# Chunk attention and two feed-forward layers on one core: 64x64 products four at a time, side work in short pieces behind steady work, GpSimd alone sums second weights, output banks rotate

## The chip, the cores and the metric

The kernel runs on one core of a Trainium2 chip. The metric is the time of one execution on the device in microseconds. Before the change it was 1657.01 us, the median of 3 runs (1655.79 to 1657.5).

## The reference

Attention is local: the 576 positions of each of 8 batches and 8 heads fall into chunks of 64, and a chunk attends to itself alone. Two feed-forward layers follow, on 4608 tokens of width 512, with 2048 hidden columns.

```python
scores = scale * np.matmul(q_c, k_c.transpose(0, 1, 2, 4, 3))   # chunks of 64 x 64
attn = np.exp(scores - max); attn = attn / (sum + 1e-09)
x = np.matmul(attn, v_c)                                         # -> [4608, 512]
h = x @ w_in;  r = np.maximum(h, 0.0);  x = (s * (r * r) + b) @ w_out
h = x @ w2_in; out = (h * (1.0 / (1.0 + np.exp(-1.702 * h)))) @ w2_out
```

The four weight matrices arrive as float64 and are turned into float32 on the chip ("decode").

## The kernel before

**Blocks and stages.** The tokens are cut into 9 blocks of 512 (`sizes`). Everything is kept transposed: features on the 128 partitions, 512 tokens in the free dimension. The first layer goes over the blocks one after the other; a block is a stage of `NS = 32` ticks, in which `gemm_in` (L479) makes 16 tiles of the hidden layer and `gemm_out` (L547), `LAG = 2` tiles behind, adds them into four accumulators in PSUM. Every product of float32 numbers is made of three matmuls on high and low parts (`split`, L94): low x high, high x high, high x low. A tile of the first layer has a steady chain behind its 12 matmuls: Relu on ScalarE (L499), s r^2 on VectorE (L500), the high part `gh` on ScalarE (L501), the low part `gl` on VectorE (L502).

**Attention.** While the first layer works on block j - 1, the four pairs of heads of block j are computed beside it (`Pair`, `plan_attention`). A pair's `steps` are a generator; `steps_at` calls `next` on it at given ticks: two 32x32 block transposes of q and k on VectorE (L252), 16 score products of 64x64 (L287), maximum and difference (L295, L296), exponential (L300), sum and quotient (L302 to L305), eight transposes (L261), 16 products with V (L271), split (L97). Float32 64x64 products take two matmuls each. Head 0 of a pair lies on partitions 0 to 63, head 1 on 64 to 127, in operands and in results. Blocks 0 and 1 are done ahead by `EarlyPair`, with transposes on TensorE, and its second product (L358) takes chunks two by two: input halves and output halves give all four combinations, and each input half has a PSUM bank of its own.

**Second weights.** The second layer runs block 0 in the same way, and the other eight two blocks at a time (`Halves`), by a scheme of seven products of quarter matrices instead of eight. For it sums and differences of quarters of the second weights are needed. `decode_second` turns a weight tile into float32 and stores it to DRAM; `sums` (L184) loads four quarters, makes four sums on GpSimd (L193 to L196), the high part on ScalarE (L198), the low part on GpSimd (L199), and stores both, 448 KB each, from SP (L204). This goes on beside the first layer in stages 2 to 8: every 13.3 ticks two decodes and two calls of `sums`.

**Halves.** The first products (`first`, L648) go through 8 tiles, with PSUM banks x (accumulator i % 4), d (the pool `at_ps`) and b; `quarter` (L668) makes the activated quarters. Then the seven output products (`second`, L742) run over 8 operands each, with both output tiles z = 0 and 1; their x banks are `acc2` and `acc3`. `operand` (L718) splits an operand (L730, L731), `result` (L763) adds, transposes and stores.

**What sets the order.** Every call is an item with a tick (`at`); the items are called in order of ticks (L885), and the framework then places the instructions on each engine's queue by a simulation of its own. A dependency without a semaphore (`tc.add_manual_dep(..., IN_ORDER)`) pins the order of two instructions on a queue. `schedule_with_timeline_sim=True` (L913) turns the simulation on. The descriptor room of GpSimd's transfers is 1024 bytes per partition (L904).

Of the kernel before, what the change touches and what calls it, by code (L numbers as in the profile page):

```python
# [11 lines left out]
ALU = mybir.AluOpType  # L12
# [12 lines left out]
FIRST_STEPS = (0, 0.6, 0.8, 1.1, 1.8, 2.4, 2.7, 3.6, 3.9, 4.5)  # L25
LAG = 2
# [18 lines left out]
def chunk_attention_two_ffn(ctx, tc, q, k, v, w1_in, w1_out, s, b, w2_in, w2_out, out):  # L45
# [33 lines left out]
    at_ps = ctx.enter_context(tc.tile_pool(name="at_ps", bufs=2, space=PSUM))  # L79
# [11 lines left out]
    wo_sums = dpool.tile([P, 7, KF // 2, 2, 2, P], F32, name="wo_sums")  # L91
    y_dram = [dpool.tile([P, KD, n], F32, name=f"y{j}") for j, n in enumerate(sizes)]
# [23 lines left out]
    def decode(st, m, c):  # L116
# [67 lines left out]
    def sums(kind, i, z):  # L184
# [3 lines left out]
        for t, (a, b) in ((i, one), (i + KF // 2, two)):  # L188
# [28 lines left out]
    heads = [slice(h * CH, (h + 1) * CH) for h in range(2)]  # L217

    class Pair:
# [20 lines left out]
        def load_v(self):  # L240
            self.v = apool.tile([P, self.nch, CH], F32, tag="vs", name="vs", bufs=HP)
            for off, m, bb, c in runs(self.j):
                for h in range(2):
                    rows = v[bb, 2 * self.hp + h, c * CH:(c + m) * CH, :]
                    nc.sync.dma_start(
                        out=self.v[h * CH:(h + 1) * CH, off:off + m, :], in_=rows.rearrange("(c p) d -> p c d", p=CH)
                    )

        def stage_qk(self):
            self.qt, self.kt = tmp("qt")[:, 0:self.n], tmp("kt")[:, 0:self.n]  # L250
            for t, src in ((self.qt, self.raw[0]), (self.kt, self.raw[1])):
                nc.vector.transpose(out=t.rearrange("p (u l) -> p u l", l=BK), in_=src)  # L252
            yield
            yield

        def turn(self, p):
            pt = tmp("pt")[:, 0:self.n].rearrange("p (c t) -> p c t", t=CH)
# [7 lines left out]
            return pt  # L265

        def second(self, pt):
            ps = at_ps.tile([P, self.n], F32, tag="at", name="xT")
            for c in range(self.nch):
                for r in heads:  # L270
                    nc.tensor.matmul(  # L271
                        out=ps[r, c * CH:(c + 1) * CH], lhsT=self.v[r, c, :], rhs=pt[r, c, :], start=True, stop=True
                    )
            return ps

        def split_x(self, ps):
            X[0, self.j, self.hp] = xh, xl = new_x()
            split(xh, xl, ps)

        def steps(self):  # L280
# [3 lines left out]
            ps = at_ps.tile([P, self.nch, CH], F32, tag="at", name="sc")  # L284
            for c in range(self.nch):
                for r in heads:
                    nc.tensor.matmul(  # L287
                        out=ps[r, c, :], lhsT=self.qt[r, c * CH:(c + 1) * CH], rhs=self.kt[r, c * CH:(c + 1) * CH],
                        start=True, stop=True,
                    )  # L290
# [4 lines left out]
            nc.vector.tensor_reduce(out=mx, in_=ps, axis=AX.X, op=ALU.max)  # L295
            nc.vector.tensor_tensor(  # L296
                out=p, in0=ps, in1=mx.unsqueeze(2).to_broadcast([P, self.nch, CH]), op=ALU.subtract
# [11 lines left out]
            turned = self.turn(p)  # L309
            yield  # L310
            ps = self.second(turned)
            yield
            self.split_x(ps)
            done[0, self.j] = done.get((0, self.j), 0) + 1

    class EarlyPair(Pair):
# [21 lines left out]
        def turn(self, p):  # L338
# [7 lines left out]
            return pt.rearrange("p (c h q) -> p c h q", h=2, q=CH)  # L346

        def second(self, pt):

            n = self.n // 2  # L350
            banks = (
                at_ps.tile([P, n], F32, tag="at", name="xT"),
                acc_ps.tile([P, n], F32, tag=f"acc{2 * (self.hp % 2) + 1}", name="xT"),
            )
            for c in range(self.nch // 2):
                for e, ps in enumerate(banks):
                    for h, r in enumerate(heads):
                        nc.tensor.matmul(  # L358
                            out=ps[r, c * CH:(c + 1) * CH],
                            lhsT=self.early.v[c][heads[e], (2 * self.hp + h) * D:(2 * self.hp + h + 1) * D],  # L360
                            rhs=pt[heads[e], c, h, :], start=True, stop=True,
                        )
            return banks

        def split_x(self, banks):
            X[0, self.j, self.hp] = x = new_x()
            xh, xl = (t.rearrange("p (c e t) -> p c e t", e=2, t=CH) for t in x)
            for e, ps in enumerate(banks):
                split(xh[:, :, e, :], xl[:, :, e, :], ps.rearrange("p (c t) -> p c t", t=CH))
            if self.j == 0:  # L370
                first_x.update((i.engine, i) for i in nc.cur_bb.bb.instructions[-2:])
            elif self.hp == HP - 1:
                marks.update((("x", i.engine), i) for i in nc.cur_bb.bb.instructions[-2:])
# [543 lines left out]
```

## Time and profile before

| | |
|---|---|
| median of 3 runs | 1657.01 us |
| the profiled execution | 1660.28 us |
| its span, first to last instruction | 1658.5 us |
| TensorE (PE) busy | 1604.2 us, 97% |
| VectorE (DVE) busy | 1149.3 us, 69% |
| ScalarE (ACT) busy | 747.0 us, 45% |
| GpSimd (POOL) busy | 266.9 us, 16% |
| mean granted clock of TensorE | 0.990 |
| chain that ended last | PE 77%, DVE 8%, DMA 4% |

A matmul's booked time reaches from its start to its modelled end, and the next one starts before that end: a full matmul is booked 0.39 us. In the rows, L12 is line 12 of the kernel before; PEld is TensorE's weight load; SPq, POOLq are the parts of engines that issue transfers. A time in brackets with an arrow is how long the engine sat idle just before, and who ended that.

### The profile page before, as it was taken

How to read it: one execution, taken by the hardware profiler on the slowest of the kernel's cores; microseconds unless marked ns; L12 is line 12 of the kernel's file. 1: busy time of each engine (PE TensorE's matmuls, PEld its weight loads, DVE VectorE, ACT ScalarE, POOL GpSimd, SP SyncE). 2: the span in 40 equal slices, each digit the busy share in tenths (PEclk: the TensorE clock that was granted, in tenths of full speed). 3: DMA queues.
4: the chain of work that ended last, by engine and by line, in shares of the span. 5: the costliest groups of instructions: out<-in, count | busy, mean ns of one | idle time of the engine just before them, and what ended most of it. 6: DMA issues, size and time to landing. Idle time of an engine off the chain costs nothing.

```text
span 1658.5 us, 24595 instructions
## 1 busy us (share of the span) xinstructions
PE 1604.2 (97%) x8928; PEld 1312.8 (79%) x8928; DVE 1149.3 (69%) x1836; ACT 747.0 (45%) x1258; POOL 266.9 (16%) x294
## 2 busy tenths in 40 slices
PE   6879999999999999999999999999999999999998
PEld 5758887778788878888888888878887888788876
DVE  5876666867687775777757543579568946984685
ACT  3768543333333333333345532456345525653552
POOL 1322101333223223233333000000001000100000
PEclk9889999999999999999999999999999999999999
DMA  9435445656455554646456441676868686767654
GB/s 229 114 102 162 121 132 131 146 132 163 122 141 145 143 136 132 156 128 155 117 160 216 135 135 45 188 239 221 206 195 266 181 221 207 255 183 218 219 192 77
DMA packets 398345, 272.19 MB, mean 164 GB/s; under 512 B 255376, under 2 KB 345488, under 8 KB 398224
## 3 DMA queue, kind: packets, MB, share of 16 engines
q1 hardware_dynamic: 390800, 249.64, 55.0%
q0 software_dynamic: 5120, 16.78, 3.0%
q10 hardware_dynamic: 2304, 4.20, 0.7%
q8 instruction: 71, 1.16, 0.3%
q14 instruction: 50, 0.41, 0.1%
HBM read 209.72 MB, written 60.82 MB: 163 GB/s over the span
## 4 chain that ended last, share of the span: by engine, by line
PE 77%; DVE 8%; DMA 4%; SPq 3%; ACT 3%; issue 2%; POOL 2%; POOLq 0%; DVEq 0%; ACTq 0%
PE acc L562 19%; PE h L487 18%; PE x L658 11%; PE x L753 11%; PE d L658 5%; PE d L753 5%; PE b L658 3%; PE b L753 3%; SPq L235 2%; PE sc L287 1%; PE xT L271 1%; DVE gl L502 1%; DVE r L500 1%; DVE pt L261 1%; ACT gh L501 1%
## 5 line engine op out<-in xcount | busy, mean ns | idle before, releaser
L487 PE MATMUL h<-xh,wi 128*128 128x512 f32 x1280 | 402.7, 396 | 13.5 <-ACT r L517 5.4
L562 PE MATMUL acc<-gh,wo 128*128 128x512 f32 x1152 | 354.8, 394 | 6.0 <-ACT gh L96 3.7
L487 PEld LDWEIGHTS h<-xh,wi 128*128 128x128 f32 x1280 | 240.3, 190 | 66.3 <-ACT r L517 6.3
L562 PEld LDWEIGHTS acc<-gh,wo 128*128 128x128 f32 x1152 | 215.5, 189 | 53.0 <-ACT gh L96 4.1
L487 PE MATMUL h<-xl,wi 128*128 128x512 f32 x640 | 251.2, 394 | 0.0
L562 PE MATMUL acc<-gl,wo 128*128 128x512 f32 x576 | 220.3, 392 | 3.8 <-DVE gl L502 3.8
L501 ACT ACTIVATE gh<-r,sb 128x512 fp32r<-128x512 f32 x112 | 80.9, 723 | 184.4 <-DVE r L500 184.1
L500 DVE SCALAR_TENSOR_TENSOR r<-r,sb 128x512 f32<-128x512 f32 x112 | 103.9, 928 | 64.3 <-ACT r L499 63.8
L502 DVE SCALAR_TENSOR_TENSOR gl<-r,sb,gh 128x512 fp32r<-128x512 f32 x112 | 107.3, 959 | 57.2 <-ACT gh L501 57.1
L487 PEld LDWEIGHTS h<-xl,wi 128*128 128x128 f32 x640 | 121.7, 190 | 25.9
L562 PEld LDWEIGHTS acc<-gl,wo 128*128 128x128 f32 x576 | 108.1, 188 | 28.6 <-DVE gl L502 6.2
L128 POOL TENSOR_TENSOR wm<-wm,wc 128x512 int32<-128x512 int32 x52 | 75.7, 1459 | 338.6 <-DVE wm L124 176.9
L730 ACT ACTIVATE op<-wo 128x512 fp32r<-128x512 f32 x128 | 79.5, 630 | 79.4 <-PE d L753 25.9
L680 DVE TENSOR_TENSOR wo<-wo,r 128x512 f32<-128x512 f32 x96 | 66.0, 691 | 63.0 <-ACT r L679 62.6
L753 PE MATMUL x<-op,wi 128*128 128x512 f32 x432 | 104.4, 389 | 0.0
L658 PE MATMUL x<-xh,wi 128*128 128x512 f32 x320 | 99.5, 391 | 3.1 <-DVE wo L677 3.1
L261 DVE STREAM_TRANSPOSE pt<-p 32x256 f32<-32x256 f32 x224 | 97.7, 436 | 3.9
L597 POOL DMA_DIRECT2D xr<-y x32 | 17.3, 540 | 506.3 <-DVE op L731 262.8
L679 ACT ACTIVATE r<-wo 128x512 f32<-128x512 f32 x96 | 60.8, 633 | 76.8 <-DVE wo L677 76.0
L753 PEld LDWEIGHTS x<-op,wi 128*128 128x128 f32 x432 | 81.1, 188 | 16.9
L731 DVE TENSOR_TENSOR op<-wo,op 128x512 fp32r<-128x512 f32 x128 | 85.2, 680 | 7.4 <-ACT op L730 6.0
L198 ACT ACTIVATE wst<-wst 128x896 fp32r<-128x896 f32 x32 | 30.5, 953 | 128.1 <-POOL wst L196 83.5
(145 smaller groups left out, 2780.1 us busy)
## 6 DMA issues: line engine op xcount, KB each, us to landing
wi<-wo_sums SPq DMA_DIRECT2D x112, 512.0 KB, 3.9
wi<-wi_sums SPq DMA_DIRECT2D x96, 512.0 KB, 3.7
wst<-in_moe_w_out SPq DMA_DIRECT2D x32, 512.0 KB, 4.6
wi_sums<-wst SPq DMA_DIRECT2D x32, 448.0 KB, 3.6
wo_sums<-wst SPq DMA_DIRECT2D x32, 448.0 KB, 3.5
wst<-in_moe_w_in SPq DMA_DIRECT2D x24, 512.0 KB, 5.0
y<-ost SPq DMA_DIRECT2D x36, 256.0 KB, 3.3
xr<-y POOLq DMA_DIRECT2D x32, 256.0 KB, 6.1
```

The lines of the kernel that those rows point to most:

```text
L128: nc.gpsimd.tensor_tensor(out=t, in0=t, in1=c.bitcast(I32), op=ALU.add)
L261: nc.vector.transpose(out=pt[r.start + ek * BK:r.start + (ek + 1) * BK, :, eq * BK:(eq + 1) * BK], in_=p[r.start + eq * BK:r.start + (eq + ...
L487: nc.tensor.matmul(out=ps, lhsT=w_[:, kk, :], rhs=x_, start=kk == 0 and a == 0, stop=kk == KD - 1 and a == 2,)
L500: nc.vector.scalar_tensor_tensor(out=r, in0=r, scalar=s_ap, in1=r, op0=ALU.mult, op1=ALU.mult)
L501: nc.scalar.activation(out=gh, in_=r, func=AF.Identity, bias=b_ap)
L502: nc.vector.scalar_tensor_tensor(out=gl, in0=r, scalar=b_ap, in1=gh.bitcast(F32), op0=ALU.add, op1=ALU.subtract)
L562: nc.tensor.matmul(out=acc[m], lhsT=l_, rhs=r_, start=i == 0 and a == 0, stop=i == KF - 1 and a == 2)
L658: nc.tensor.matmul(out=self.ps[key], lhsT=l_, rhs=r_, start=start and k == 0 and a == 0, stop=k == HK - 1 and a == 2, skip_group_check=not ...
L680: nc.vector.tensor_tensor(out=g, in0=h, in1=r, op=ALU.mult)
L730: nc.scalar.activation(out=hi, in_=src, func=AF.Copy)
L731: nc.vector.tensor_tensor(out=lo, in0=src, in1=hi.bitcast(F32), op=ALU.subtract)
L753: nc.tensor.matmul(out=self.ps[key], lhsT=l_, rhs=r_, start=start and i == 0 and a == 0, stop=i == HF - 1 and a == 2, skip_group_check=not ...
```

## The change

- **Products.** `quarters` gives the 16 products of a pair in an order in which four follow each other on the four combinations of input half and output half. Half of the chunks (e = 1) get the other output half; V is loaded with its halves exchanged for them. Scores and xT lie in halves (`left`, `right`) of two banks that are held for the whole kernel (`at_banks`). The early pairs' scores are done the same way.
- **Side work.** The transposes of a pair become single steps (q, k) and four steps of two; `PAIR_STEPS` gives 13 ticks. Every instruction that a `step` issues on ScalarE or VectorE gets a dependency without a semaphore on the latest steady instruction (Relu, s r^2, gh, gl) whose tick has passed.
- **Decode.** The square on ScalarE and the multiplication with the mask come before GpSimd's add instead of after it; the add is last.
- **sums.** The high part is made by GpSimd, the low part in four pieces, and both stores are issued by GpSimd.
- **Banks.** The d banks are the two of `at_banks` in turn; the x banks of `first` and of the outputs begin at accumulator 0 or 2 in turn (`turn`).
- **The end.** In the last pair of blocks the last product is ordered by output tile: from operand 2 on, first all of z = 0, then all of z = 1.

```diff
+PAIR_STEPS = (-2, -1.5, -1, 1, 1.9, 2.2, 3, 3.7, 4.2, 4.7, 5.2, 8, 8.5)
-    at_ps = ctx.enter_context(tc.tile_pool(name="at_ps", bufs=2, space=PSUM))
+    at_ps = ctx.enter_context(tc.tile_pool(name="at_ps", bufs=1, space=PSUM))
+    at_banks = at_ps.tile([P, 2, NB_MAX], F32, name="at")
     (decode)
+        square = low.bitcast(F32)
+        nc.scalar.activation(out=square, in_=high.bitcast(F32), func=AF.Square)
+        nc.vector.scalar_tensor_tensor(out=m, in0=square, scalar=TINY * TINY, in1=m, op0=ALU.is_ge, op1=ALU.mult)
+        yield
         nc.gpsimd.tensor_tensor(out=t, in0=t, in1=c.bitcast(I32), op=ALU.add)
-        nc.scalar.activation(out=c, in_=high.bitcast(F32), func=AF.Square)
-        yield
-        nc.vector.scalar_tensor_tensor(out=m, in0=c, scalar=TINY * TINY, in1=m, op0=ALU.is_ge, op1=ALU.mult)
     (sums)
-        nc.scalar.activation(out=hi, in_=q[:, 1:8, :], func=AF.Copy)
-        nc.gpsimd.tensor_tensor(
-            out=q[:, 1:8, :].bitcast(F32R), in0=q[:, 1:8, :], in1=hi.bitcast(F32), op=ALU.subtract
-        )
+        nc.gpsimd.tensor_copy(out=hi, in_=q[:, 1:8, :])
+        for t0, t1 in ((0, 2), (2, 4), (4, 6), (6, 7)):
+            nc.gpsimd.tensor_tensor(
+                out=q[:, 1 + t0:1 + t1, :].bitcast(F32R), in0=q[:, 1 + t0:1 + t1, :], in1=hi[:, t0:t1, :].bitcast(F32),
+                op=ALU.subtract,
+            )
-            nc.sync.dma_start(out=to[:, :, part, :], in_=src)
+            nc.gpsimd.dma_start(out=to[:, :, part, :], in_=src)
     (products of a pair)
+    left, right = at_banks[:, :, 0:NB_MAX // 2], at_banks[:, :, NB_MAX // 2:NB_MAX]
+    def quarters(nch):
+        for i in range(nch // 2):
+            for e in range(2):
+                for h in range(2):
+                    yield e, i, e * (nch // 2) + i, h, heads[h], heads[h ^ e]
     (Pair.load_v)
+                for e in range(2):
+                    a, z = max(off, e * half), min(off + m, (e + 1) * half)
+                    for h in range(2) if a < z else ():
+                        rows = v[bb, 2 * self.hp + h, (c + a - off) * CH:(c + z - off) * CH, :]
+                        nc.sync.dma_start(
+                            out=self.v[heads[h ^ e], a:z, :], in_=rows.rearrange("(c p) d -> p c d", p=CH)
+                        )
     (Pair.second; the scores likewise, into left)
-            ps = at_ps.tile([P, self.n], F32, tag="at", name="xT")
-            for c in range(self.nch):
-                for r in heads:
+            for e, i, c, h, r, other in quarters(self.nch):
+                nc.tensor.matmul(
+                    out=right[r, e, i * CH:(i + 1) * CH], lhsT=self.v[other, c, :], rhs=pt[other, c, :],
+                    start=True, stop=True,
+                )
     (Pair.turn: a yield after every two transposes; plan_attention)
-            steps_at(((o - 2, 3), (o + 1, 1), (o + 2, 4), (o + 8, 1), (o + 8.5, 1)), pr.steps)
+            steps_at([(o + t, 1) for t in PAIR_STEPS], pr.steps)
     (EarlyPair)
+        def room_scores(self):
+            return right if self.j == 0 and self.hp % 2 else left
     (gemm_in, first layer from block 2 on)
+        def steady(d, engine):
+            served.append((NS * j + 2 * i + d, engine, nc.cur_bb.bb.instructions[-1]))
             nc.scalar.activation(out=r, in_=ps, func=AF.Relu)
+            steady(2, ACT)
             nc.vector.scalar_tensor_tensor(out=r, in0=r, scalar=s_ap, in1=r, op0=ALU.mult, op1=ALU.mult)
+            steady(2.2, DVE)
     ...  (gh: 2.6, gl: 2.8)
     (Halves)
+            self.turn = j // 2 * HK % KD
+            if bank == "d":
+                self.ps[key] = at_banks[:, next(turns) % 2, :]
+                return
-                self.bank(key, BANK[m], f"acc{i % KD}")
+                self.bank(key, BANK[m], f"acc{(self.turn + i) % KD}")
-                    self.bank(key, BANK[m], f"acc{HK + z}")
+                    self.bank(key, BANK[m], f"acc{(self.turn + z) % KD}")
+                    if self.last and n == len(OUT_ORDER) - 1 and i >= 2:
+                        for z in range(2):
+                            at(base + 4 * n + 1 + 1.5 * z + 0.25 * (i - 2), self.second, n, i, (z,))
     (the loop over the items)
+        for ins in traced[n:] if f.__name__ == "step" else ():
+            first = next((g for u, e, g in reversed(served) if u <= t and e == ins.engine), None)
+            if first is not None:
+                tc.add_manual_dep(ins, first.name, IN_ORDER, reason="behind the tile before")
```

## Rows read from the trace of the kernel before

**Rows 1.** Page, part 1: busy time, share of the span, instructions of each engine.

```profile
PE 1604.2 (97%) x8928; PEld 1312.8 (79%) x8928; DVE 1149.3 (69%) x1836; ACT 747.0 (45%) x1258; POOL 266.9 (16%) x294
```

**Rows 2.** Busy time by stretches; columns as the first line says.

```profile
core 0: us, PE busy (x) PEld busy (x) DVE busy (x) ACT busy (x) POOL busy (x), PEclk, DMA share, GB/s
40.00:120.00 80.00, 64.14 (x515) 50.44 (x515) 64.26 (x108) 55.06 (x102) 24.13 (x17) 0.87 0.40 110
200.00:640.00 440.00, 429.72 (x2834) 349.53 (x2832) 320.67 (x519) 164.30 (x263) 115.82 (x129) 1.00 0.56 140
320.00:360.00 40.00, 37.77 (x266) 30.33 (x265) 24.90 (x36) 13.16 (x21) 13.14 (x15) 0.96 0.59 144
1120.00:1160.00 40.00, 40.00 (x178) 33.15 (x177) 40.00 (x68) 24.98 (x45) 0.01 (x1) 1.00 0.68 220
280.00:860.00 580.00, 572.60 (x3770) 469.55 (x3770) 429.23 (x681) 210.79 (x335) 184.67 (x206) 1.00 0.54 138
```

**Rows 3.** Waits of PE, 200:900 and 1000:1660: us in total, times, longest.

```profile
PE h L487 <- ACT r L499: 4.2, 3, 2.2
PE acc L562 <- DVE gl L502: 3.8, 3, 1.4
PE acc L562 <- ACT gh L501: 2.1, 3, 0.9
...
PE x L753 <- DVE wo L680: 5.8, 4, 1.5
```

**Rows 4.** Timeline of PE at 346 and 118: start us, us, instructions.

```profile
346.29 1.15 PE L271 MATMUL xT<-pt,vs 64*64 64x64 f32 x32
347.37 0.73 PE L487 MATMUL h<-xh,wi 128*128 128x512 f32 x2
...
118.22 0.69 PE L358 MATMUL xT<-pt,wo 64*64 64x64 f32 x32
118.85 0.73 PE L562 MATMUL acc<-gh,wo 128*128 128x512 f32 x2
```

**Rows 5.** Groups by line, PE: count | busy us, mean ns | idle before.

```profile
L287 PE MATMUL sc<-kt,qt 64*64 64x64 f32 x1152 | 45.7, 232 | 0.5 <-ACT kt L336 0.5
...
L271 PE MATMUL xT<-pt,vs 64*64 64x64 f32 x896 | 33.8, 221 | 0.0
```

**Rows 6.** Timeline of all engines at 337 to 339, and of VectorE at 269.

```profile
337.52 0.95 ACT L198 ACTIVATE wst<-wst 128x896 fp32r<-128x896 f32 x1 [9.94 <-POOL wst L196]
...
338.54 2.10 POOL L199 TENSOR_TENSOR wst<-wst 128x896 fp32r<-128x896 f32 x1 [1.06 <-ACT wst L198]
338.99 2.21 DVE L500 SCALAR_TENSOR_TENSOR r<-r,sb 128x512 f32<-128x512 f32 x1 [5.90 <-ACT r L499]
...
339.00 0.73 PE L487 MATMUL h<-xh,wi 128*128 128x512 f32 x2 [2.23 <-ACT r L499]
...
269.79 3.59 DVE L261 STREAM_TRANSPOSE pt<-p 32x256 f32<-32x256 f32 x8
```

**Rows 7.** Waits of all engines: us in total, times, longest.

```profile
ACT wst L198 <- POOL wst L196: 83.5, 18, 9.9
```

**Rows 8.** Groups by line, POOL: count | busy us, mean ns | idle before.

```profile
L199 POOL TENSOR_TENSOR wst<-wst 128x896 fp32r<-128x896 f32 x32 | 68.1, 2129 | 50.0 <-ACT wst L198 50.0
L194 POOL TENSOR_TENSOR wst<-wst 128x128 f32<-128x128 f32 x32 | 21.2, 663 | 83.9 <-DMA wst<-w_wi 37.5 <-DMA wst<-w_wo 35.7 <-DMA ks<-in_k 6.7
...
L597 POOL DMA_DIRECT2D xr<-y x32 | 17.3, 540 | 506.3 <-DVE op L731 262.8 <-ACT r L679 136.5 <-DVE wo L147 39.1
```

**Rows 9.** Timeline at 1133 to 1136, PE and VectorE.

```profile
1133.11 3.11 PE L753 MATMUL x<-op,wi 128*128 128x512 f32 x13
...
1133.44 0.68 DVE L731 TENSOR_TENSOR op<-wo,op 128x512 fp32r<-128x512 f32 x1
```

**Rows 10.** Timeline of the end: VectorE, then SP's issues.

```profile
1650.81 1.40 DVE L772 STREAM_TRANSPOSE ost<-x 128x512 f32<-128x512 f32 x2 [6.60 <-PE x L753]
...
1651.56 4.14 SPq L776 DMA_DIRECT2D out<-ost  x8
```

More of the change, by code (lines that the diff above doesn't have):

```diff
@@ L1 @@
+from itertools import count
 import concourse.bass as bass
@@ L241, in load_v @@
             self.v = apool.tile([P, self.nch, CH], F32, tag="vs", name="vs", bufs=HP)
+            half = self.nch // 2
             for off, m, bb, c in runs(self.j):
[L243 to L247, printed above, removed]
+                for e in range(2):
[5 more added lines that the diff above has]
+                        )
         def stage_qk(self):
@@ L264, in turn, with split_x @@
                         )
-            return pt
+                    yield
+        def room_scores(self):
+            return left
         def second(self, pt):
-            ps = at_ps.tile([P, self.n], F32, tag="at", name="xT")
-            for c in range(self.nch):
-                for r in heads:
[L271 to L278, printed above, removed]
+            for e, i, c, h, r, other in quarters(self.nch):
[3 more added lines that the diff above has]
+                )
+        def split_x(self):
+            X[0, self.j, self.hp] = x = new_x()
+            split(*(t.rearrange("p (e n) -> p e n", e=2) for t in x), right)
         def steps(self):
@@ L283, in steps @@
             yield
[L284 to L290, printed above, removed]
+            ps = self.room_scores().rearrange("p e (c t) -> p e c t", t=CH)
+            for e, i, c, h, r, other in quarters(self.nch):
+                nc.tensor.matmul(
+                    out=ps[other, e, i, :], lhsT=self.qt[r, c * CH:(c + 1) * CH], rhs=self.kt[r, c * CH:(c + 1) * CH],
+                    start=True, stop=True,
+                )
             yield
@@ L294, in steps @@
             p = tmp("p")[:, 0:self.n].rearrange("p (c t) -> p c t", t=CH)
-            nc.vector.tensor_reduce(out=mx, in_=ps, axis=AX.X, op=ALU.max)
+            by_bank = mx.rearrange("p (e c) -> p e c", e=2)
+            nc.vector.tensor_reduce(out=by_bank, in_=ps, axis=AX.X, op=ALU.max)
             nc.vector.tensor_tensor(
-                out=p, in0=ps, in1=mx.unsqueeze(2).to_broadcast([P, self.nch, CH]), op=ALU.subtract
+                out=p.rearrange("p (e c) t -> p e c t", e=2), in0=ps,
+                in1=by_bank.unsqueeze(3).to_broadcast([P, 2, self.nch // 2, CH]), op=ALU.subtract,
             )
@@ L308, in steps @@
             yield
-            turned = self.turn(p)
+            yield from self.turn(p)
+            self.second(self.pt)
             yield
-            ps = self.second(turned)
-            yield
-            self.split_x(ps)
+            self.split_x()
             done[0, self.j] = done.get((0, self.j), 0) + 1
@@ L345, in turn, with room_scores @@
             nc.vector.tensor_copy(out=pt, in_=ps)
-            return pt.rearrange("p (c h q) -> p c h q", h=2, q=CH)
+            self.pt = pt.rearrange("p (c h q) -> p c h q", h=2, q=CH)
+            yield
+        def room_scores(self):
+            return right if self.j == 0 and self.hp % 2 else left
         def second(self, pt):
             n = self.n // 2
[L351 to L354, printed above, removed]
+            if self.j == 0:
+                self.ps = (
+                    h_ps.tile([P, n], F32, tag="h", name="xT"),
+                    acc_ps.tile([P, n], F32, tag=f"acc{2 * (self.hp % 2) + 1}", name="xT"),
+                )
+            else:
+                self.ps = right[:, 0, :], right[:, 1, :]
             for c in range(self.nch // 2):
-                for e, ps in enumerate(banks):
+                for e, ps in enumerate(self.ps):
                     for h, r in enumerate(heads):
+                        of = h ^ (c >= self.nch // 4)
                         nc.tensor.matmul(
@@ L360, in second, with split_x @@
                             lhsT=self.early.v[c][heads[e], (2 * self.hp + h) * D:(2 * self.hp + h + 1) * D],
-                            rhs=pt[heads[e], c, h, :], start=True, stop=True,
+                            rhs=pt[heads[e], c, of, :], start=True, stop=True,
                         )
-            return banks
-        def split_x(self, banks):
+        def split_x(self):
             X[0, self.j, self.hp] = x = new_x()
[L367 to L373, printed above, removed]
+            xh, xl = (t.rearrange("p (c e t) -> p e c t", e=2, t=CH) for t in x)
+            if self.j:
+                split(xh, xl, right.rearrange("p e (c t) -> p e c t", t=CH))
+                if self.hp == HP - 1:
+                    marks.update((("x", i.engine), i) for i in nc.cur_bb.bb.instructions[-2:])
+                return
+            for e, ps in enumerate(self.ps):
+                split(xh[:, e], xl[:, e], ps.rearrange("p (c t) -> p c t", t=CH))
+            first_x.update((i.engine, i) for i in nc.cur_bb.bb.instructions[-2:])
     class Early:
@@ L504, in gemm_in @@
             )
+            steady(2.8, DVE)
         else:
@@ L580, in chunk_attention_two_ffn @@
     HF, HK = KF // 2, KD // 2
+    turns = count()
     def minus(to, one, two):
@@ L585, in chunk_attention_two_ffn, with __init__ @@
     class Halves:
-        def __init__(self, j, base):
-            self.j, self.base = j, base
+        def __init__(self, j, base, last):
+            self.j, self.base, self.last = j, base, last
+            self.turn = j // 2 * HK % KD
             self.x, self.w, self.g, self.op, self.ps, self.kept = {}, {}, {}, {}, {}, {}
@@ L740, in chunk_attention_two_ffn, with second @@
         n_ops = 0
-        def second(self, n, i):
+        def second(self, n, i, sides=(0, 1)):
             m = OUT_ORDER[n]
-            hi, lo = self.op.pop((n, i))
+            hi, lo = self.op[n, i]
             w = self.wo[n, i // 2]
-            for z in range(2):
+            for z in sides:
                 key = "out", z, BANK[m]
```

17 lines of the change are left out of this document (10 added, 7 removed).

## The prediction, written before the changed kernel ran

> **What bounds the kernel now.** I read the page's first part, then the busy time by stretches, then who waited for whom, and last the timeline around each loss. TensorE is busy for 97% of the span [rows 1], and a dense stretch without attention work holds 178 full matmuls in 40 us, 0.2247 us each [rows 2]. So TensorE sets the end: an edit pays only if it takes time out of TensorE's stream or closes a hole in it. The holes: 15.9 us idle in 40:120, at a granted clock of 0.87; 10.3 us in 200:640, and within it a clock of 0.96 in 320:360 [rows 2]; and four waits of 1.5 us late in the kernel [rows 3]. VectorE's 69% is no bound as a mean, but in 1120:1160 it is busy for all of the 40 us [rows 2]; there it decides what a closed hole is worth.
>
> **A. 64x64 products four at a time.** Before, the products run two at a time: 32 matmuls (16 products, two passes each) stand between a start at 346.29 and the next full matmul at 347.37, 1.08 us [rows 4]. The second product of the early pairs already uses all four quarters of the array: its 32 at 118.22 take 0.69 instead of 1.15 us, and the next full matmul starts at 118.85, 0.63 later [rows 4]. This is the shape that the change gives to every product; the difference is 0.45 us a block. There are 896 / 32 = 28 blocks of xT and 1152 / 32 = 36 of scores, of which 8 belong to early pairs [rows 5]: 56 blocks in the dense part, each in TensorE's own stream with nothing beside it, so **-25.2 us**. Bounds: 0 (they run as pairs after all; a loss is out, as count and kind of instructions stay) and -25.2. I take the full value, since the row has the same operand sizes.
>
> The Trainium skill speaks against it ("TensorE: Matmul & The Clock Gate", section "Wait — 56ns, not 53.3ns?"): starts of matmuls never come closer than about 25 ns, however small they are. By it 32 starts need 0.8 us and A shrinks to some -7 us (an estimate). The row differs: 32 in 0.69 us, with 0.22 for the last, is 15 ns between starts [rows 4, 5]; I go by the row.
>
> What A needs beside it costs nothing. V's halves change partitions, so `load_v` issues at most six loads a pair where it issued four: two more of SP's half microseconds (D) in the 20 us of a pair, while SP hands 64 stores of 448 KB to GpSimd. Scores and xT get one buffer each, in halves of the same two banks, and are used again a pair later: 7 ticks of 3 us (a stage of 32 ticks is 384 full matmuls and eight blocks, 95 us), where max, subtract and split hold them for 0.7 us each. Even if the banks are guarded whole, a reader waits for one block, and TensorE is back 7 ticks later.
>
> **B. Side work: `sums` on GpSimd alone, decode without a round trip, short pieces.** The timeline of the largest hole shows the chain [rows 6]: ScalarE's copy L198 stands 9.94 us at the head of its queue for GpSimd's sums; the Relu L499 comes behind it; then VectorE's L500 takes 2.21 us because GpSimd's L199 (2.10) runs across it; and TensorE waits 2.23 us. In all, L198 waited 83.5 us for GpSimd [rows 7]. After the change no instruction of `sums` or of the second weights' decode makes ScalarE or VectorE wait for GpSimd's result, so this blocking goes. The other kind is a run of VectorE steps, eight transposes for 3.59 us ahead of steady work [rows 6]; they become four pieces with steady work ordered ahead of them.
>
> The size: 10.3 us idle, 0.04 x 40 = 1.6 for the clock [rows 2], and the hidden part of nine waits [rows 3] (a full matmul is booked 0.39 busy and spaced 0.225, so 0.16 each, 1.4): 13.3. The new order starts with the first tile of stage 2, so the holes around that tile (240:280) are not all in its reach; I leave 2.3 of them. **-11 us**, bounds 0 and -13.3.
>
> What is late next is GpSimd. A `sums` step costs it four small sums of at most 0.66 [rows 8], 2.6 us; the subtraction in four pieces, 3.2 (L199's 2.13, and 0.36 for each extra start: a small sum has the columns of a seventh of L199, 0.30); one copy that no row shows on this engine, between 0.3 (a seventh of L199) and 2.13 (L199 itself, the same columns with two inputs): I take 2.1, the same shape; and two stores. A 256 KB transfer of 128 rows is issued in 0.54 [rows 8]; these have 896 rows, so between 0.54 and seven times that, 3.8; I take 1. Sum 9.9 us. Every 13.3 ticks (39 us) bring two `sums` and two decodes (an add, about 1.5 by its columns against L199, and an issue): 2 x 9.9 + 2 x 2.0 = 24 us. It fits, and at 3.8 an issue it is 35. Behind a store on GpSimd stand the next add and the next sums; their readers come stages later. GpSimd's hold on VectorE stays as long in sum, in pieces of 0.5 to 0.8 us, the copy at worst 2.1.
>
> The new order adds no semaphore, but a step of a pair now stands behind the Relu, square, gh or gl of the tile due before it. Behind the step stand the pair's later steps, and TensorE waits for them at two points: scores come 2.5 ticks after the second transpose of q and k, xT 2.8 ticks after the last transpose of p, 7 to 8 us of cover for steady operations of 0.75. VectorE is 429 of 580 us busy in 280:860 [rows 2], 79% once the stretch is 36 us shorter: the cover holds.
>
> **C. Output banks rotate.** Where first products give way to second ones, TensorE waits four times, 5.8 us in all, for L680 [rows 3], the last reader of the second output bank. With the banks alternating the outputs take the two that were read two tiles earlier. But VectorE is full behind it: the tightest operand that I find is ready at 1133.44 + 0.68 = 1134.12, and the matmul that reads it is the last of the 13 from 1133.11, near 1135.83 [rows 9]: 1.7 us of slack, of which 1.5 will be used. It fits barely. **-5.2 us**, bounds 0 (VectorE takes it back) and -6.4 (with 0.16 hidden each).
>
> **D. The end.** VectorE's last two transposes end at 1652.2, and SP's last eight issues take 4.14 us from 1651.56, 0.52 each [rows 10]; z = 1 gets its turn after the four of z = 0, near 1653.6. With z = 0 finished 18 matmuls (4 us) earlier its issues are over, and z = 1 starts near 1652.3. **-1.3 us**, bounds 0 and -2.1 (four issues).
>
> **E. The first 120 us.** The eight blocks of early scores get shorter by 0.45 us or, at half clock, twice that, and the first weights' decode loses ScalarE's square behind GpSimd's add. But 15.9 us of idle there [rows 2] belong to many waits in a row. Bounds -5 (a third of the idle) and +3 (one hole like the largest, with its clock); **-1.5**.
>
> Sum: -25.2 - 11 - 5.2 - 1.3 - 1.5 = -44.2. The profiled execution took 1660.28 us (span 1658.5 and 1.8 around it), so 1616.1 in its terms; the median of the runs shown is 1657.01, 3.3 less: **1613 us**.
>
> **The rivals.**
> 1. The holes move: pieces and order make the pair's own chain late, and VectorE takes C back; B and C bring nothing. For it: VectorE's full stretch, and 79%. Against: 7 us of cover. 1613 + 16 = 1629.
> 2. The change doesn't do what it says: four products, two from different row halves into one bank, fall back to pairs. For it: the block at 118.22 gives each bank one row half only. Against: the pairs before already write one bank from both. 1613 + 25 = 1638. The Trainium skill ("TensorEngine Tiling (Array Packing)", "Gotcha 1: PSUM Pressure") says that row tiles can't use one bank at the same moment; no row here shows such a loss.
> 3. Starts stay nearer to the pairs' 30 ns, (1.15 - 0.22) / 31, than to 15 [rows 4]: halfway, A is halved, 1626.
> 4. GpSimd becomes the bound, and the kernel slower: a store of 896 rows holds its queue, sums come late, staging rooms stay taken, SP stands before them, and q and k land late. Without its four stores a period needs 2 x 7.9 + 2 x 2.0 = 20 of 39 us, so it decides from 4.8 us a store; at 6.5 the period is 46, and 16 of them cost 112: 1725. Against: seven times the row is 3.8.
>
> **How the numbers follow.** Forecast 0.61, rival 1 0.17, rival 2 0.06, rival 3 0.05, rival 4 0.07, better than 1600 (every upper bound) 0.04. The range 1600 to 1638 holds the forecast with its bounds and rivals 1 to 3. A measurement of this kernel tells 0.2%, 3.3 us, from no change: faster 0.93, within 0.02, slower 0.05, the last two from rival 4.
>
> **What would show it.** A: groups of 32 small products near 0.7 us. B: no wait of ScalarE for GpSimd in `sums`, and under 3 us of TensorE's waits in 280:860. C: no wait at the four changes and none for operands soon after. D: four issues behind the last transpose. Wrong if a block keeps 1.1 us, if GpSimd needs over 4 us for a store, or if TensorE waits for the operands of scores or xT.

## The result and the profile after

The changed kernel takes 1680.69 us, the median of 4 runs (1676.39 to 1685.72), against 1656.4 for the kernel before, now with a fourth run: a ratio of 1.0146 [1.013, 1.0163], 1.5% slower, and the whole interval lies above 1. 1613 had been forecast. The profiled execution has a span of 1674.4 us, 15.9 more than before.

Where the 15.9 us arise can be read from TensorE's own milestones, the first matmul of a stage in the timeline: up to stage 2 it is 1.6 us later than before (209.35 against 207.74); stages 2 to 8, the first layer with attention and side work beside it, take 755.0 us instead of 730.2 (+24.8); from there to the last matmul it is 704.4 instead of 713.5 (-9.0); and behind the last matmul 5.56 instead of 7.06 (-1.5). One stretch made the change slower, and it is the one in which most of the gain was to lie.

The page's first line of the changed kernel, for [rows 1]:

```profile
PE 1588.8 (95%) x8928; PEld 1287.1 (77%) x8928; DVE 1158.0 (69%) x1832; ACT 716.2 (43%) x1222; POOL 398.9 (24%) x486
```

GpSimd works half as long again as before, and is idle for 76% of the span all the same. The busy time by stretches, for [rows 2]; the columns are engines' busy us with their instructions, then the granted clock:

```profile
320.00:340.00 20.00, 18.29 (x127) 15.19 (x128) 17.90 (x30) 4.85 (x8) 7.31 (x11) 0.83 0.47 114
280.00:860.00 580.00, 545.60 (x3681) 436.78 (x3680) 415.78 (x664) 175.48 (x289) 282.06 (x357) 0.98 0.49 131
```

In 280:860 TensorE idles 34.4 us where it idled 7.4, and GpSimd is busy for 282 of 580 us, 49%, so it has time left. TensorE's waits in 200:930 of the changed kernel (us in total, times, longest), for [rows 3]:

```profile
PE acc L607 <- DVE gl L546: 10.1, 11, 1.6
...
PE acc L607 <- ACT gh L544: 8.6, 6, 4.6
...
PE acc L607 <- DVE ost L615: 7.6, 6, 3.1
...
PE h L528 <- ACT r L540: 6.3, 4, 2.3
...
PE at L296 <- DVE pt L285: 6.0, 5, 2.3
```

With two small ones they are 41.1 us in 34 waits, against 10.1 in 9 before [rows 3]. All of them wait for ScalarE or VectorE. What held those two stands in the waits of all engines over the same stretch, sorted by time:

```profile
ACT wc L125 <- DMA wst<-in_moe_w_in: 75.3, 13, 13.5
DVE wm L126 <- DMA wst<-in_moe_w_in: 70.3, 10, 16.0
ACT wc L125 <- DMA wst<-in_moe_w_out: 50.0, 11, 9.5
POOL wi_sums L213 <- issue: 43.1, 15, 5.0
DVE wm L126 <- DMA wst<-in_moe_w_out: 40.6, 12, 6.4
POOL wo_sums L213 <- issue: 34.6, 13, 4.0
```

L125 and L126 are the decode's first instructions on ScalarE and VectorE. They waited 236 us for their loads. In the same stretch of the kernel before, one wait for such a load is listed:

```profile
DVE wm L121 <- DMA wst<-in_moe_w_in: 0.2, 1, 0.2
```

Why the loads come late is in SP's waits (whole kernel):

```profile
SPq L119 <- DMA wi_sums<-wst: 57.2, 8, 13.0
...
SPq L113 <- DMA wo_sums<-wst: 51.9, 10, 10.8
```

SP holds the decode's load (L113, L119) until a store of `sums` has landed. A load goes into a staging room (`staged`, three in all, and one call of `sums` takes two), and the room is free only when the store out of it is through. These are 109.1 us; the kernel before has 10.8 of the same kind:

```profile
SPq L108 <- DMA wo_sums<-wst: 6.2, 8, 1.7
...
SPq L114 <- DMA wi_sums<-wst: 4.6, 8, 0.7
```

One event from the timeline of all engines (start, us, instruction, and in brackets the idle time ahead of it with its releaser):

```profile
679.90 2.31 SPq L256 DMA_DIRECT2D qs<-in_q  x3
...
685.91 0.90 POOL L213 DMA_DIRECT2D wo_sums<-wst  x1
...
689.54 0.39 SPq L113 DMA_DIRECT2D wst<-in_moe_w_in  x1
...
689.79 0.91 POOL L213 DMA_DIRECT2D wo_sums<-wst  x1 [2.49 <-issue]
...
693.74 0.67 ACT L125 ACTIVATE wc<-wst 128x512 int32<-128x512 uint32 x1 [13.53 <-DMA wst<-in_moe_w_in]
693.75 0.43 DVE L126 TENSOR_SCALAR wm<-wst 128x512 int32<-128x512 int32 x1 [16.00 <-DMA wst<-in_moe_w_in]
...
694.82 0.75 DVE L542 SCALAR_TENSOR_TENSOR r<-r,sb 128x512 f32<-128x512 f32 x1
...
695.61 0.72 ACT L544 ACTIVATE gh<-r,sb 128x512 fp32r<-128x512 f32 x1 [0.44 <-DVE r L542]
...
696.38 1.22 PE L607 MATMUL acc<-gh,wo 128*128 128x512 f32 x2 [4.61 <-ACT gh L544]
```

SP's next issue after 682.2 is the decode's load at 689.54. It lands at 693.7, and only then the heads of ScalarE's and VectorE's queues move, which have stood for 13.5 and 16 us. Behind them stand s r^2 (L542) and `gh` (L544) of a tile, and TensorE loses 4.61 us. This load was let go by the landing of the first store, issued at 685.91 without a wait. The second store is issued 2.49 us late, at 689.79, without any wait that the profile shows, and is not what held this load. Such waits stand further back in the same chain:

```profile
657.60 0.90 POOL L213 DMA_DIRECT2D wi_sums<-wst  x1 [2.99 <-issue]
...
661.54 0.58 POOL L183 DMA_DIRECT2D w_wo<-wm  x1 [1.73 <-issue]
...
664.00 0.80 SPq L196 DMA_DIRECT2D wst<-w_wo  x2
```

The second store of the call before and, behind it, the store of a decode (L183) come 2.99 and 1.73 us late. SP stands 13.0 us until that decode's store has landed, and only then issues, at 664.00, the first loads (L196) for the sums that are stored at 685.91.

GpSimd's operations one by one, for [rows 8] (count, busy us and mean ns, then the idle time before them):

```profile
L207 POOL TENSOR_TENSOR wst<-wst 128x256 fp32r<-128x256 f32 (+1 forms) x128 | 111.0, 897 | 1.4
...
L204 POOL CAST wst<-wst 128x896 fp32r<-128x896 f32 x32 | 33.9, 1059 | 57.0 <-DMA wi_sums<-wst 29.1 <-DMA wo_sums<-wst 26.9
L213 POOL DMA_DIRECT2D wi_sums<-wst x32 | 28.9, 902 | 46.1 <-issue 43.1 <-DVE wm L129 3.0
L213 POOL DMA_DIRECT2D wo_sums<-wst x32 | 28.9, 902 | 43.7 <-issue 41.1 <-DMA vs<-in_v 2.6
```

The decode's own stores, 32 of 256 KB behind the add, wait the same way, 39.9 us in all:

```profile
L183 POOL DMA_DIRECT2D w_wi<-wm x16 | 9.2, 575 | 22.7 <-issue 19.8 <-POOL wm L137 2.9
L183 POOL DMA_DIRECT2D w_wo<-wm x16 | 9.1, 569 | 23.2 <-issue 20.1 <-POOL wm L137 3.1
```

All 44 of these waits, 30 at L213 and 14 at L183, end 0.3 us after GpSimd's transfer before has landed.

And what went as forecast, in the timeline of TensorE (for [rows 4]) and in its waits in 1000:1660 (for the last line of [rows 3]):

```profile
647.83 0.69 PE L296 MATMUL at<-pt,vs 64*64 64x64 f32 x32
648.46 0.73 PE L528 MATMUL h<-xh,wi 128*128 128x512 f32 x2
```

```profile
PE x L805 <- ACT gh L782: 1.3, 4, 0.3
```

A block of 32 small products takes 0.63 us instead of 1.08, and the four waits at the change from first to second products are 0.3 us each instead of 1.5.

### The profile page after: what moved, and what is told of

Its sections match the earlier page's. It is cut to its first block, busy times and chain, and to the rows that moved or that the text cites. A ratio compares the mean times of both kernels' runs of the same rounds, so it can differ in the third digit from the quotient of the medians.

```text
span 1674.4 us, 24713 instructions
## 1 busy us (share of the span) xinstructions
PE 1588.8 (95%) x8928; PEld 1287.1 (77%) x8928; DVE 1158.0 (69%) x1832; ACT 716.2 (43%) x1222; POOL 398.9 (24%) x486
## 4 chain that ended last, share of the span: by engine, by line
PE 51%; DVE 12%; DMA 12%; POOL 10%; issue 7%; SPq 6%; ACT 2%; POOLq 0%; DVEq 0%; ACTq 0%
PE x L805 10%; PE x L710 9%; PE acc L607 8%; PE h L528 7%; PE at L805 5%; PE at L710 5%; POOL wst L207 4%; SPq L256 3%; PE b L805 3%; PE b L710 3%; DMA wo_sums<-wst 2%; DMA wi_sums<-wst 2%; SPq L196 1%; POOL wm L137 1%; DVE r L542 1%
## 5 line engine op out<-in xcount | busy, mean ns | idle before, releaser
L607 PE MATMUL acc<-gh,wo 128*128 128x512 f32 x1152 | 359.3, 398 | 18.9 <-ACT gh L544 8.6
L528 PEld LDWEIGHTS h<-xh,wi 128*128 128x128 f32 x1280 | 240.8, 190 | 69.2 <-ACT r L562 10.4
L607 PE MATMUL acc<-gl,wo 128*128 128x512 f32 x576 | 222.9, 397 | 10.3 <-DVE gl L546 10.1
L544 ACT ACTIVATE gh<-r,sb 128x512 fp32r<-128x512 f32 x112 | 80.9, 723 | 230.3 <-DVE r L542 230.0
L546 DVE SCALAR_TENSOR_TENSOR gl<-r,sb,gh 128x512 fp32r<-128x512 f32 x112 | 101.7, 909 | 45.3 <-ACT gh L544 44.9
L207 POOL TENSOR_TENSOR wst<-wst 128x256 fp32r<-128x256 f32 (+1 forms) x128 | 111.0, 897 | 1.4
L542 DVE SCALAR_TENSOR_TENSOR r<-r,sb 128x512 f32<-128x512 f32 x112 | 102.1, 912 | 8.1 <-ACT r L540 7.5
L126 DVE TENSOR_SCALAR wm<-wst 128x512 int32<-128x512 int32 x52 | 24.2, 472 | 111.0 <-DMA wst<-in_moe_w_in 70.3
```

The lines of the kernel that those rows point to most:

```text
L207: nc.gpsimd.tensor_tensor(out=q[:, 1 + t0:1 + t1, :].bitcast(F32R), in0=q[:, 1 + t0:1 + t1, :], in1=hi[:, t0:t1, :].bitcast(F32), op=ALU.s ...
L528: nc.tensor.matmul(out=ps, lhsT=w_[:, kk, :], rhs=x_, start=kk == 0 and a == 0, stop=kk == KD - 1 and a == 2,)
L542: nc.vector.scalar_tensor_tensor(out=r, in0=r, scalar=s_ap, in1=r, op0=ALU.mult, op1=ALU.mult)
L544: nc.scalar.activation(out=gh, in_=r, func=AF.Identity, bias=b_ap)
L546: nc.vector.scalar_tensor_tensor(out=gl, in0=r, scalar=b_ap, in1=gh.bitcast(F32), op0=ALU.add, op1=ALU.subtract)
L607: nc.tensor.matmul(out=acc[m], lhsT=l_, rhs=r_, start=i == 0 and a == 0, stop=i == KF - 1 and a == 2)
```

## The experiments

All ratios are against the kernel before, which ran on the same chip beside them (medians 1656.2 to 1657.3). The edits are to the changed kernel.

**1. SP issues the stores.**

```diff
-            nc.gpsimd.dma_start(out=to[:, :, part, :], in_=src)
+            nc.sync.dma_start(out=to[:, :, part, :], in_=src)
```

> Changed kernel, but the two stores of sums are issued by SP again. Theory (room): the loss sits where the load of a decode waits for a staging room that a store of sums, issued late by GpSimd, still holds, while ScalarE and VectorE stand at L125/L126 for that load; stores from SP leave right behind the subtraction, so these waits (236 us of the two engines in all) at least halve and the time falls from 1681 to 1625-1655. Rival 1 (the pinned order makes side work stiff): 1670-1690, as before. Rival 2 (GpSimd's copy and pieces are simply too much work): 1665-1690.

1627.1 us, 0.9825 [0.9811, 0.984]. That one word is worth 53.6 us. The same views of this kernel, the busy time in 280:860 and the decode's waits in 200:930:

```profile
280.00:860.00 580.00, 575.65 (x3874) 468.13 (x3873) 435.01 (x705) 199.10 (x327) 251.68 (x332) 1.00 0.58 149
```

```profile
DVE wm L126 <- DMA wst<-in_moe_w_in: 35.5, 9, 9.1
ACT wc L125 <- DMA wst<-in_moe_w_in: 33.8, 12, 8.4
ACT wc L125 <- DMA wst<-in_moe_w_out: 28.2, 7, 7.0
DVE wm L126 <- DMA wst<-in_moe_w_out: 17.6, 7, 4.0
```

They are 115 us, half of the 236, and TensorE idles 4.4 us of the 580. What is computed on GpSimd is unchanged, so the loss was in who issues the stores.

**2. GpSimd issues them, with twice the descriptor room.**

```diff
-dynamic_dma_scratch_size=1024
+dynamic_dma_scratch_size=2048
```

> Changed kernel with 2048 instead of 1024 bytes per partition of descriptor room for GpSimd's transfers. Theory (room), if the 84 us that GpSimd waits for nothing visible ahead of L213 are descriptor room: these waits fall under 20 us, the load of the decode comes some 3 to 5 us sooner, time 1645-1670. If those waits are something else, or by rivals 1 and 2: unchanged, 1674-1688.

1637.71 us, 0.9886 [0.9866, 0.9906]: 43.0 of the 53.6 us come back, more than expected. The stores in this kernel:

```profile
L213 POOL DMA_DIRECT2D wo_sums<-wst x32 | 29.9, 958 | 0.0
L213 POOL DMA_DIRECT2D wi_sums<-wst x32 | 29.8, 955 | 0.1
```

An issue takes 0.96 us instead of 0.90, and the 84 us ahead of it are gone; so are the 39.9 ahead of the decode's stores. So a transfer right behind another had waited for room for its descriptors. SP still stands 84.5 us for staging rooms (109.1 in the changed kernel) and the decode's heads 163 (236); TensorE's waits in 200:930 are 14.4 us instead of 41.1.

**3. The first store is issued earlier**, behind the copy that makes the high part and ahead of the four pieces, in the room of 1024 bytes.

```diff
         nc.gpsimd.tensor_copy(out=hi, in_=q[:, 1:8, :])
+        nc.gpsimd.dma_start(out=to[:, :, 0, :], in_=hi.bitcast(F32))
     ...
-        for part, src in enumerate((hi.bitcast(F32), q[:, 1:8, :])):
-            nc.gpsimd.dma_start(out=to[:, :, part, :], in_=src)
+        nc.gpsimd.dma_start(out=to[:, :, 1, :], in_=q[:, 1:8, :])
```

> Changed kernel, stores still on GpSimd with 1024 bytes of descriptor room, but the store of the high part is issued right behind the copy, ahead of the four subtractions (some 3 us), so the two stores of a call are no longer back to back. Theory (descriptor room: a store of 896 rows takes nearly all of it, the second waits for the first to drain): GpSimd's waits ahead of L213 fall from 84 us to under 35 and the time from 1681 to 1637-1662. If GpSimd's stores are slow for another reason (their landing, their count): 1670-1690.

1631.42 us, 0.9857 [0.9835, 0.988]. That is 6 us better than the expected range. L213 waits 14.1 us in 200:930 instead of 77.7, the decode's heads 86 instead of 236, TensorE 10.7 instead of 41.1. The decode's own stores still wait 42.5 us and SP still stands 77.5 us for staging rooms (4.9 in run 1): those two alone cost little. The same stores on the same engine with the same room cost 4 us more than SP's, and not 54, when 3.5 us of other work lie between them.

**4. No pins** (the dependency of side work on the steady instruction before it is left out).

```diff
-        for ins in traced[n:] if f.__name__ == "step" else ():
+        for ins in traced[n:] if f.__name__ == "unpinned" else ():
```

> Changed kernel without the added order (no step is pinned behind the steady work of a tile). Rival 1 (stiff order): the holes of stages 2 to 8 go, 1620-1645. Theory (room): the decode is still queued ahead of its data, so the time stays within 12 us, 1670-1695.

1684.8 us, 1.0173 [1.0155, 1.0191]. L213 waits 76.3 us and the decode's heads 236, as in the changed kernel. The stiff order is not the cause.

**5. The decode's second step later**, so that its instructions reach the heads of the queues when the load is there.

```diff
-steps_at(((t, 1), (t + 2.0, 1)), ... decode_second(kind, i))
+steps_at(((t, 1), (t + 4.5, 1)), ... decode_second(kind, i))
     (the second decode of the period likewise)
```

> Changed kernel, but the second step of a second weight's decode comes 4.5 instead of 2 ticks after its load is called, that is 2.5 ticks (7.5 us) later; nothing on GpSimd changes. Theory (room): ScalarE and VectorE no longer stand at L125/L126 for most of the 236 us; 1630-1660. Rival 1: unchanged, 1670-1690. Rival 2: unchanged or worse.

1704.5 us, 1.0292 [1.0276, 1.0308]: the expectation was wrong, and the sign too. The heads wait longer still, 274 us, and so does SP, in 200:930 of this kernel (129.4 us for the first two rows and 111.6 for the last two, against 109.1 and 102.9 in the changed kernel):

```profile
SPq L119 <- DMA wi_sums<-wst: 66.5, 10, 12.1
SPq L113 <- DMA wo_sums<-wst: 62.9, 10, 14.2
SPq L196 <- DMA w_wo<-wm: 58.7, 12, 7.9
SPq L196 <- DMA w_wi<-wm: 52.9, 9, 7.2
```

The side work is a loop: a room, the load into it, the decode, its store, the loads of `sums` (L196), the sums, their stores, the room. A later decode makes the next round's rooms free later. That reading fits the rows; no other run isolates it.

**6. The sums as before** (ScalarE makes the high part, GpSimd subtracts once over 896 columns, SP stores); decode, pins, products and banks as changed.

```diff
-        nc.gpsimd.tensor_copy(out=hi, in_=q[:, 1:8, :])
+        nc.scalar.activation(out=hi, in_=q[:, 1:8, :], func=AF.Copy)
-        for t0, t1 in ((0, 2), (2, 4), (4, 6), (6, 7)):
+        for t0, t1 in ((0, 7),):
-            nc.gpsimd.dma_start(out=to[:, :, part, :], in_=src)
+            nc.sync.dma_start(out=to[:, :, part, :], in_=src)
```

> Changed kernel with sums as before the change: high part by ScalarE, one subtraction of 128x896 on GpSimd, both stores from SP. It tells what GpSimd alone is worth once the stores are off its queue (1627 with SP's stores). Theory: ScalarE again stands behind GpSimd's sums for some 80 us and the holes of before return, 1633-1645. Rival (the pins alone had closed them): 1622-1630.

1623.35 us, 0.9806 [0.9791, 0.982], outside the theory's 1633 to 1645 and inside the rival's. Taking the sums off ScalarE was worth nothing beside the pins. ScalarE's wait for GpSimd, 83.5 us before [rows 7], and the decode's loads in this kernel:

```profile
ACT wst L204 <- POOL wst L202: 17.8, 6, 4.8
DVE wm L126 <- DMA wst<-in_moe_w_in: 9.3, 5, 2.5
ACT wc L125 <- DMA wst<-in_moe_w_in: 8.8, 6, 4.4
```

**7. Sums as before, and no pins** (edits of 6 and 4).

> Sums as before and no pins; the decode's order, the fours and the rotating banks of the change stay. What made the holes of [rows 6] go, with the sums back on ScalarE? Theory A (the pins and short pieces closed them, as the prediction had it for the side work in general): the holes come back, worth the prediction's 11 us at most, so 1628 to 1635. Theory B (the pins are worth as little here as beside SP's stores, 1.9 us, and the holes went with the 64x64 products, whose shorter bursts leave ScalarE's tiles more slack): 1622 to 1627.

1644.88 us, 0.9929 [0.9914, 0.9945], slower than either theory had it. ScalarE stands for GpSimd again:

```profile
ACT wst L204 <- POOL wst L202: 87.9, 21, 8.2
```

Here the pins are worth 21.5 us, more than the holes of the kernel before held: TensorE idles 14.3 us in 280:860 (565.74 busy) where it idled 7.4. Why the new pieces do worse without pins than the old steps did was not tried. **8. SP's stores and no pins** (edits of 1 and 4) gives their worth with the sums on GpSimd:

> Stores from SP, and no step pinned behind a tile's steady work. If the pins do what the prediction gave them (cover against runs of side work): slower than 1627 by 3 to 12 us. If the order comes out alike by the simulation anyway: 1625-1630.

1629.04 us, 0.9842 [0.9825, 0.9858], 1.9 us above run 1 with intervals that overlap. With run 6 (the pins alone) and run 7 (neither) this says that either the pins or GpSimd alone (with SP's stores) closes the holes of [rows 6]; the change did both, and the second cost more than it could bring.

**9. SP's stores and the decode in its old order** (the add first, then the square and the mask).

```diff
-        square = low.bitcast(F32)
-        nc.scalar.activation(out=square, in_=high.bitcast(F32), func=AF.Square)
     ...
         nc.gpsimd.tensor_tensor(out=t, in0=t, in1=c.bitcast(I32), op=ALU.add)
+        nc.scalar.activation(out=c, in_=high.bitcast(F32), func=AF.Square)
```

> Stores from SP, decode with GpSimd's add in the middle as before the change. It tells whether the decode's new order makes the start late (stage 2 begins 3.5 us later than before the change) and what it gives in stages 2 to 8. Theory: the start comes back by 2 to 4 us, stages 2 to 8 lose 0 to 6: 1624-1632. Rival (the start is late because of the early pairs, not the decode): start unchanged, 1627-1634.

1624.49 us, 0.9813 [0.9796, 0.983]: the old order is 2.6 us better than the new one in run 1, but the intervals overlap. Stage 2 begins at 210.2, so the late start was not brought back.

**10. Sums as before, output banks not in turn.**

```diff
-f"acc{(self.turn + i) % KD}"
+f"acc{i % KD}"
-f"acc{(self.turn + z) % KD}"
+f"acc{HK + z}"
```

> Sums as before, and the output banks no longer rotate; the rest of the change stays. Theory (the rotation is worth the 2.2 us for each of four pairs of blocks that the traces show between before and after, in the last stage): 8 to 10 us more than the 1623.4 of the old sums, so 1631 to 1634. Rival (the last stage got faster through the side work leaving it, not through the banks): within 2 us of 1623.4.

1629.49 us, 0.9835 [0.9818, 0.9852], 6.1 above run 6, and 5.3 by the traces (709.7 against 704.4 from stage 9 to the last matmul): less than the theory's 8 to 10, and more than the rival's 2. The four waits are back to the tenth in 940:1660:

```profile
PE x L805 <- DVE wo L732: 5.8, 4, 1.5
```

**11. Sums as before, small products in pairs:** only the loops change places.

```diff
-        for i in range(nch // 2):
-            for e in range(2):
+        for e in range(2):
+            for i in range(nch // 2):
```

> Sums as before, and the order of the small products alone is put back: e is the outer loop, so that the same two quarters of TensorE follow each other and only two products can run beside each other. Theory (the order is what makes fours of pairs): blocks of small products take 1.1 to 1.2 and 2.1 us again, 20 to 25 us more than 1623.4, so 1643 to 1649. Rival (the smaller tiles or their placing made them fast, or half of the time is hidden behind other work): 1625 to 1637.

1634.01 us, 0.9861 [0.9842, 0.988]: 10.7 us above run 6, half of what the theory expected and inside the rival's range. A block in this kernel:

```profile
628.52 0.98 PE L296 MATMUL at<-pt,vs 64*64 64x64 f32 x32
629.43 0.72 PE L528 MATMUL h<-xh,wi 128*128 128x512 f32 x2
```

It takes 0.91 us, between 1.08 and 0.63. For a block that stands alone, as here, the order is worth 0.28 of the 0.45 us. Where two blocks follow each other, they take 1.50 us together (from 566.22 to 567.72), against 2.01 in the kernel before (574.25 to 576.26) and 1.09 in run 6: 0.41 of 0.92. Over all small products from 205 us on, the time up to the next full matmul is 56.9 us before, 45.2 here and 33.2 in run 6, so the order is worth half of the gain, 12 of 24 us. The other half came with the rest of the edit to the products, such as the placing of operands and results (two banks instead of one), which no run undid.

**12. Sums and decode as before, the rest as changed:** the version that the runs point to.

> Sums as in the kernel before (ScalarE takes the high parts, one GpSimd subtraction, SP stores) and decode in the old order; pins, fours and rotating banks of the change stay. Theory (GpSimd's part of the change only costs, decode's new order too, and the two costs add): 1623.4 of the old sums less the 2.6 us that the old decode gave beside SP's stores (1627.1 to 1624.5), so 1619 to 1622. Rival (both remove the same wait, ScalarE and VectorE standing at the decode's heads): 1623 to 1625, no gain over the old sums alone.

1620.2 us, 0.9784 [0.9766, 0.9802], 3.1 us below run 6: the lowest of all, 36 us below the kernel before. The step from run 6 is not shown, as the intervals overlap; of the 4.6 us between the two traces 3.5 are the start of stage 2 (207.7 against 211.2), which varies without a known reason (E below).

## Why the prediction was wrong

**Right.** A: a block takes 0.63 instead of 1.08 us, the 0.45 of the forecast, so some 24 to 25 us left TensorE's stream; in run 6 stages 4 to 6 take 92.71 us each, where they took 96.4, 98.4 and 96.7. Rivals 2 and 3 fell with that row. The Trainium skill's floor of about 25 ns between starts ("TensorE: Matmul & The Clock Gate", section "Wait — 56ns, not 53.3ns?") doesn't hold for this shape: (0.69 - 0.22) / 31 is 15 ns. The estimate of some -7 us by that floor was itself a little small: 31 intervals shorter by 5 ns, in 56 blocks, are about 9 us. C: 5.2 forecast, 5.3 by run 10; the last stages gained 9.0. Of the other 3.7, 3.1 are four waits of the kernel before that are gone, in run 10 too:

```profile
PE x L658 <- DVE wo L677: 3.1, 4, 0.8
```

VectorE did not take it back. D: 1.5 us, 1.3 forecast.

**Off.** E: +1.6 us instead of -1.5. Stage 2 began between 207.4 and 211.3 us over the variants, with no edit that goes with it (run 9 has the old decode and begins late, run 7 the new one and begins at 207.5). It is open.

**Wrong: B.** Stages 2 to 8 should have lost A's 25 and B's 11 us, and took 24.8 more: B is about +50 instead of -11. The rows carry that: 31 us of added waits; 25 more of them with 0.16 hidden in each, 4; and the granted clock, 9: it is 0.83, 0.91, 0.91, 0.90 and 0.93 in five stretches of 20 us and 1.00 in the others, which loses 10.4 us, against 1.6 before. Together they are 44; the other 6 are not accounted for. The clock fell where the waits stand: in 320:340 the mean is 0.83, so for part of those 20 us the lower level, 1.2 GHz, was granted; TensorE had waited there for 0.9 and then 2.3 us, up to 321.7. One sign that the prediction had named for being wrong came too: TensorE waited 6.0 us in five waits for xT's operands (L296), and 0.2 in run 1.

The step that failed is the sentence "Behind a store on GpSimd stand the next add and the next sums; their readers come stages later." It looked at readers of results, and placed them stages away. There are nearer ones. The add's result is read by the next sums of the same period: SP stood 102.9 us in 200:930 for the decode's stores (L196), 90.7 before. And what a store of `sums` leaves is a room, which the next load of a decode takes: SP, which issues in order, stood 109.1 us for it, 10.8 before, and behind that load the heads of ScalarE and VectorE stand still. The earlier claim, that nothing in `sums` or decode makes these two engines wait for GpSimd's result, holds by the letter, as ScalarE's 83.5 us [rows 7] are gone, and helped nothing: they waited 236 us for loads instead, 115 when SP issued the stores (run 1) and 29 with the old sums (run 6). The program before showed the two steps: SP's stores from the same rooms, and three rooms of which a call of `sums` takes two.

The runs show that GpSimd's issuing of the stores is the cause (run 1), and that nearly all of it is the wait ahead of them (runs 2 and 3). How that wait reaches TensorE, through the rooms or through late adds and sums, no run separates. SP's standing alone doesn't decide it: in runs 2 and 3 it stands 84.5 and 77.5 us for rooms, and the loss is nearly gone.

The costs themselves were nearly right. A call of `sums` takes 2.34 us for the four small sums (0.59 each), 1.06 for the copy, 3.47 for the pieces and 1.80 for two stores: 8.7 us, 9.9 forecast. A store is issued in 0.90 us, where 1 was taken. What no term held is the wait for descriptor room that run 2 shows: 84.2 us over 64 stores of `sums`, and 39.9 over the 32 of the decode. The Trainium skill ("DMA: Bandwidth & Descriptors", section "SWDGE vs HWDGE vs iDMA") says that GpSimd writes its descriptors to rings in SBUF while SP's are made in hardware. Runs 1 and 2 agree: neither has the wait. It gives no size from which a store would stand.

Rival 4 named the mechanism (rooms taken, SP standing) and lost by its price: it was to decide from 4.8 us a store, because it let GpSimd's throughput decide. With the wait a store costs 0.90 + 84.2 / 64 = 2.2 us, GpSimd is busy for 49% of 280:860, and the loss is there. Its victim was another too: not q and k, but the decode's loads at the heads of two queues. Rival 1 (the holes move through pieces and order) is out: without the pins the loss stays (run 4), and with pins and pieces but SP's stores TensorE idles 4.4 us in 280:860 (run 1).

And the gain that B was to bring was smaller. In run 6, without the loss, stages 2 to 8 take 701.7 us, 28.6 less than before: A's 24 to 25 and some 3 to 5 for the holes, not 11: TensorE's waits in 200:930 are still 6.3 us in 5, against 10.1 in 9. With 3.5 for B the forecast would have been about 1621; run 12 took 1620.2. That it comes so near is luck in part: the last stages gave 3.8 us more than C, and E nothing of its 1.5.

## What to carry to other kernels

When a step moves to another queue, follow what it gives free as closely as what it computes: list who takes the buffer next, on which in-order queue that load stands, and what stands behind its first reader. Where GpSimd issues two transfers right behind each other, look in the trace for idle time with no releaser ahead of the second; work between them, more descriptor room or SP as the issuer took it away here. And when two edits cure the same hole, price the second at nothing until a run says otherwise.

## What the runs showed of the hardware

- A store of 448 KB from 128 partitions (896 rows of 512 bytes) is issued by GpSimd in 0.90 us. With 1024 bytes of descriptor room per partition the stores of `sums` waited up to 5.0 us ahead of their issue, 84.2 us over 64 of them, and each of these waits ended 0.3 us after GpSimd's transfer before had landed; with 2048 bytes they waited 0.1 us in all.
- On GpSimd a copy with conversion of 128x896 took 1.06 us, half of the 2.14 of a subtraction of the same shape (run 6). In pieces, 128x256 or 128x128, the same subtraction took 3.47 us.
- 64x64 products that follow each other on four quarters of the array start 15 ns apart ((0.69 - 0.22) / 31), also where both input halves write one bank, at different partitions.
